# Cross network on one Trainium2 core: first rows in four transfers over two queues, biases on GpSimd's queue, small turns later

## The chip, the cores and the metric

The kernel runs on one core of one Trainium2 chip. A core has five engines with instruction streams of their own: TensorE (PE, matrix products into PSUM, with weight loads shown apart as PEld), VectorE (DVE), ScalarE (ACT), GpSimd (POOL) and SyncE (SP, which here only issues transfers). They wait for each other through semaphores. SP, ACT and GpSimd can issue DMA transfers between the chip's memory and the core's SBUF. The metric is device time of one execution in microseconds (us), the median of several runs.

## The reference

```python
B, F, D, L = 4096, 26, 16, 6
Din = min(F * D, 1024)                      # 416
# x0: (4096, 416), ws: (6, 416, 416), bs: (6, 416), all bfloat16
def reference(x0, ws, bs):
    x = x0
    for l in range(ws.shape[0]):
        x = x0 * (x @ ws[l] + bs[l]) + x
    return x
```

Six cross layers on 4096 rows of 416 features. Each layer is one 416 x 416 product per row, a bias, a product with the input and a sum.

## The kernel before

The kernel keeps x transposed: features on the 128 partitions, rows along the free dimension. The 416 features are cut into three blocks of 128 (called c, or k as an input and m as an output) and a tail of 32. The 4096 rows are done in NP = 4 passes of 1024, each pass in two blocks of NB = 512 rows. The tails of all 1024 rows of a pass are packed into one tile of 128 x 256, four groups of 32 partitions. A pass goes through the six layers; n = p * L + l counts the 24 steps. In every step TensorE does the products of block 0 (`main(p, l, 0, n)`), the tail's (`tail`, lines 433 to 485) and those of block 1; VectorE adds the bias and multiplies by x0 (L606, L615), with ScalarE (L708) and GpSimd (L290) doing one of the six chunks between them. The sum with x is folded into PSUM: the products of a pass's layers accumulate there, so x0 * (sum + bias) is the next x. The last step (`last`) turns the result so that rows are on the partitions.

The change touches the start, where nothing is in SBUF yet. There the order is written out by hand on each engine:

- **Loading.** Rows 0 to 511 (block 0 of pass 0) come as they lie in memory, in `xin_sb`, four groups j = 0 to 3 of 128 rows. SP loads groups 0 and 1 in one transfer (L162), ACT groups 2 and 3 in another (L648). Then SP issues the weights of layer 0 in three transfers (L166, semaphores `s_w0[k]`), a transposing load of rows 512 to 1023 (L169, `s_x0[0]`), waits for the third weights, and goes on with the weights of the later layers (L174, L178). ACT goes on with the tails of rows 512 to 1023 (L651, `xtb_sb`), the biases (L655, `bsa_sb`, after GpSimd has filled that tile with ones) and the tail's weight rows of layer 0 (L656, `w3_sb`).
- **Constants.** GpSimd makes `ones_sb`, `bsa_sb`, the identity `ident`, `u_sb` and a zeroed `wc_sb` (L245 to L256), then packs the tails into `xtn_sb` (L261, two copies, counted by `s_xtp`), copies the tail biases (L270, `s_bs4`) and builds the block-diagonal `wc_sb` (L277).
- **TensorE.** `idle(28)` issues 28 products of a constant (L309) whose result nobody reads. Then `first()` turns `xin_sb` by column block: for c = 0, 1, 2 the four groups j (L321), waiting for the two loads in c = 0; `at(c, j)` names the PSUM bank. `s_inT` counts what is ready: both halves of c = 0, then c = 1, then c = 2. Then come the products of layer 0 for k = 0, 1, 2 (L381, four each, 512 or 256 columns), each k after its weights and after VectorE's copy of that column block. Behind k = 0 stand the two small turns, which transpose the packed tails (L353), and the four bias products (`biases`, L332), which put the biases of all layers on the partitions. `tail` of step 0 (L458, then L391 and L479) waits for the copied tails, `cb_sb`, the full `w3_sb` and, ahead of L479, for the transposing load.
- **VectorE.** Four copies of the turned blocks (L580, `s_ev` 1 to 4), the copy of the turned tails (L585, `s_ev` 5) and two half copies of it (L588, `s_dup`), the copy of the biases to `cb_sb` (L590, `s_cb`), and a copy inside `w3_sb` (L595, `s_w30`). Then the steps.

## Time and profile before

| | us |
|---|---|
| median of 3 runs | 129.04 (128.87 to 129.15) |
| the profiled execution's own time | 128.59 |
| its span, first to last instruction | 126.8 |
| TensorE busy | 123.3 (97%) |
| VectorE busy | 93.3 (74%) |
| ScalarE busy | 45.1 (36%) |
| GpSimd busy | 32.1 (25%) |

The profile records one execution. The time of an execution is a little longer than its span, since it takes in what lies around the instructions. In the views a line of the timeline gives start, length, engine, line of the kernel, operation, what it writes and reads, and the number of instructions merged into it; "SPq" and "ACTq" are instructions that issue transfers. The chain is the work that ended last, followed back from the end. "L321" is line 321 of the kernel before; most line numbers behind the change differ from it in the kernel after.

### The profile page before, as it was taken

What the parts mean: (1) busy time and instruction counts of PE and PEld (TensorE: products, weight loads), DVE (VectorE), ACT (ScalarE), POOL (GpSimd) and SP (SyncE); (2) the same over time, 40 slices, a digit from 0 to 9 for tenths busy, and PEclk for the clock granted to TensorE, in tenths of its full rate; (3) what the DMA queues carried; (4) which work ended last, traced back from release to release, by engine and by line L of the source; (5) the groups of instructions that cost most, each with busy time, mean ns of one, the idle gap of its engine ahead of it and who ended that gap; (6) DMA issues with size and microseconds to landing.
All of it is one profiled execution on the core that took longest, in us unless ns stands there. A gap on an engine that the chain in (4) does not pass through costs nothing.

```text
span 126.8 us, 5809 instructions
## 1 busy us (share of the span) xinstructions
PE 123.3 (97%) x2930; PEld 65.7 (52%) x2403; DVE 93.3 (74%) x156; ACT 45.1 (36%) x99; POOL 32.1 (25%) x42
## 2 busy tenths in 40 slices
PE   7999999999999999999999999999999999999991
PEld 7754554554554554555445545545545545545571
DVE  0567967868869769669669679688687696696873
ACT  0544724625422413403404314224214224135720
POOL 5351311312303303303303213123033033033040
PEclk9999999999999999999999999999999999999999
DMA  3969999597899304907001968000000768000017
GB/s 106 255 157 309 203 119 169 68 100 171 246 120 153 60 16 82 177 20 254 0 16 20 119 130 269 5 0 5 5 10 16 139 114 269 5 0 5 0 53 221
DMA packets 35623, 13.27 MB, mean 105 GB/s; under 512 B 26986, under 2 KB 35600, under 8 KB 35600
## 3 DMA queue, kind: packets, MB, share of 16 engines
q1 hardware_dynamic: 33912, 12.07, 48.4%
q10 hardware_dynamic: 1688, 0.83, 2.5%
q8 instruction: 21, 0.34, 1.1%
q14 instruction: 2, 0.02, 0.0%
HBM read 3.99 MB, written 3.41 MB: 58 GB/s over the span
## 4 chain that ended last, share of the span: by engine, by line
PE 95%; DVE 3%; DVEq 0%; issue 0%
PE ps L391 62%; PE ps L371 11%; PE ps L458 8%; PE ps L479 6%; PE ps L381 4%; PE ps L309 2%; DVE o_sb L635 2%; PE ps L321 1%; PE ps L552 0%; DVE o_sb L641 0%; DVE x0t_sb L585 0%; DVEq L41 0%; PE ps L353 0%; DVEq L632 0%
## 5 line engine op out<-in xcount | busy, mean ns | idle before, releaser
L606 DVE SCALAR_TENSOR_TENSOR xT_sb<-ps,cb_sb,x0T_sb 128x512 bf16<-128x512 f32 x100 | 69.3, 743 | 22.1 <-PE ps L458 22.1
L391 PE MATMUL ps<-xT_sb,w_sb 128*32 128x512 bf16 (+1 forms) x1380 | 75.7, 343 | 0.0
L391 PEld LDWEIGHTS ps<-xT_sb,w_sb 128*32 128x32 bf16 x1380 | 36.9, 97 | 35.3 <-issue 8.1
L290 POOL TENSOR_TENSOR xT_sb<-t_sb,x0T_sb 128x512 bf16<-128x512 f32 x20 | 23.3, 1163 | 72.1 <-ACT t_sb L708 72.1
L708 ACT ACTIVATE t_sb<-ps,cb_sb 128x512 f32<-128x512 f32 x23 | 15.8, 687 | 59.1 <-PE ps L458 59.1
L371 PE MATMUL ps<-xT_sb,w_sb 128*32 128x256 bf16 x444 | 26.6, 273 | 0.0
L672 ACT ACTIVATE xt_sb<-xt_sb 64x256 bf16<-64x256 bf16 x38 | 15.8, 415 | 9.8 <-DVE xt_sb L615 9.3
L391 PE MATMUL ps<-x0T_sb,w_sb 128*32 128x512 bf16 (+1 forms) x252 | 14.1, 344 | 0.0
L606 DVE SCALAR_TENSOR_TENSOR xo_sb<-ps,cb_sb,x0T_sb 128x512 bf16<-128x512 f32 x15 | 10.4, 744 | 3.3 <-PE ps L458 3.3
L391 PEld LDWEIGHTS ps<-x0T_sb,w_sb 128*32 128x32 bf16 x252 | 6.7, 97 | 6.5 <-issue 1.5
L458 PE MATMUL ps<-xt_sb,w_sb 32*128 32x256 bf16 x228 | 9.6, 271 | 0.0
L479 PE MATMUL ps<-xT_sb,w_sb 128*32 128x256 bf16 x228 | 9.5, 273 | 0.0
L615 DVE SCALAR_TENSOR_TENSOR xt_sb<-ps,cb_sb,x0t_sb 128x256 bf16<-128x256 f32 x20 | 9.5, 474 | 0.0
L458 PEld LDWEIGHTS ps<-xt_sb,w_sb 32*128 32x128 bf16 x228 | 4.2, 92 | 6.2 <-issue 6.1
L290 POOL TENSOR_TENSOR xo_sb<-t_sb,x0T_sb 128x512 bf16<-128x512 f32 x3 | 3.5, 1166 | 11.2 <-ACT t_sb L708 11.2
L479 PEld LDWEIGHTS ps<-xT_sb,w_sb 128*32 128x32 bf16 x228 | 6.1, 97 | 0.1
L391 PE MATMUL ps<-xt_sb,wc_sb 128*32 128x256 bf16 x76 | 5.6, 283 | 0.0
L381 PE MATMUL ps<-w_sb,xT_sb 128*128 128x416 bf16 (+2 forms) x27 | 5.2, 320 | 0.0
L666 ACT ACTIVATE wc_sb<-w_sb 32x32 bf16<-32x32 bf16 x20 | 4.5, 226 | 1.6 <-DMA w_sb<-in_ws_dram 1.2
L371 PE MATMUL ps<-x0T_sb,w_sb 128*32 128x256 bf16 x84 | 5.0, 273 | 0.0
L580 DVE COPY x0T_sb<-ps 128x256 bf16<-128x256 bf16 (+1 forms) x4 | 1.3, 356 | 4.3 <-PE ps L321 4.3
L391 PEld LDWEIGHTS ps<-xt_sb,wc_sb 128*32 128x32 bf16 x76 | 1.9, 92 | 4.0 <-issue 4.0
(56 smaller groups left out, 49.8 us busy)
## 6 DMA issues: line engine op xcount, KB each, us to landing
out_dram<-o_sb SPq DMA_DIRECT2D x3, 832.0 KB, 4.2
w_sb<-in_ws_dram SPq DMA_DIRECT2D x5, 312.0 KB, 5.9
xr_sb<-in_x_dram SPq DMA_DIRECT2D x1, 832.0 KB, 6.1
w_sb<-in_ws_dram SPq DMA_DIRECT2D x5, 104.0 KB, 3.2
out_dram<-o_sb SPq DMA_DIRECT2D x2, 208.0 KB, 2.1
w_sb<-in_ws_dram ACTq DMA_DIRECT2D x3, 104.0 KB
xin_sb<-in_x_dram SPq DMA_DIRECT2D x1, 208.0 KB, 2.9
xin_sb<-in_x_dram ACTq DMA_DIRECT2D x1, 208.0 KB, 3.2
```

What stands on the lines that cost most here:

```text
L290: pool.tensor_tensor(out=xdst(p, l, 0, 2), in0=t_sb[:, n % 2, :], in1=x0c(p, 0, 2), op=ALU.mult,).then_inc(s_pl, 1)
L309: pe.matmul(ps[:, 0, 0:128], lhsT=ones, rhs=ones, start=True, stop=True)
L371: return pe.add_instruction(mybir.InstMatmult(name="I-%d" % (1000000 + count[0]), engine=mybir.EngineType.PE, start_tensor_calc=start, sto ...
L381: return pe.matmul(out, lhsT=lhsT, rhs=rhs, start=start, stop=stop, skip_group_check=True)
L391: ins = pe.matmul(out[c:c + 32, :], lhsT=lhsT[:, c:c + 32], rhs=rhs, start=start, stop=stop, skip_group_check=True, tile_position=(0, c),)
L458: ins = pe.matmul(part(blk, m, h ^ other), lhsT=w3_sb[32 * g:32 * g + 32, l, m * 128:(m + 1) * 128], rhs=xt[32 * g:32 * g + 32, other, :], ...
L479: ins = pe.matmul(ps_tail[32 * g:32 * g + 32, :], lhsT=w_sb[:, l, k, DF:D], rhs=xsrc(p, l, g % 2, k)[:, (g // 2) * NT:(g // 2 + 1) * NT], ...
L606: dve.scalar_tensor_tensor(out=halves(xdst(p, l, blk, c)), in0=chunk2(blk, c), scalar=cb_sb[:, c, l:l + 1], in1=halves(x0c(p, blk, c)), op ...
L615: dve.scalar_tensor_tensor(out=tdst(p, l), in0=ps_tail, scalar=cb_sb[:, 3, l:l + 1], in1=x0t_sb[:, p, 0, :], op0=ALU.add, op1=ALU.mult,).t ...
L666: act.activation(out=wc_sb[gs, l, gs], in_=w3_sb[gs, l, DF:D], func=ACTF.Copy).then_inc(s_wc, 1)
L672: act.activation(out=o, in_=i, func=ACTF.Copy).then_inc(s_dup, 1)
L708: act.activation(out=halves(t_sb[:, n % 2, :]), in_=chunk2(0, 2), func=ACTF.Identity, bias=cb_sb[:, 2, l:l + 1],).then_inc(s_act, 1)
```

## The change

The first 512 rows come in four transfers of 128 rows, groups 0 and 2 on SP and 1 and 3 on ACT, each with a semaphore of its own, ahead of everything else on these queues. TensorE issues 23 products of the constant instead of 28 and turns by group: groups 0 and 1 in all three column blocks as they land, then groups 2 and 3 block by block. The biases are loaded from GpSimd's queue, right after GpSimd has filled their tile with ones and ahead of its other constants. The two small turns move from behind k = 0 to the middle of k = 1, the bias products behind k = 1. On VectorE the copy inside `w3_sb` comes ahead of the copy to `cb_sb`.

```diff
-        s_xin = [sem("s_xin%d" % i) for i in range(2)]
+        s_xin = [sem("s_xin%d" % i) for i in range(4)]
...
         def _(sp):
-            sp.dma_start(
-                xin_sb[:, 0:2, :], x0[0:256, :].rearrange("(j b) d -> b j d", b=128)
-            ).then_inc(s_xin[0], 16)
+            for j in (0, 2):
+                sp.dma_start(xin_sb[:, j, :], x0[j * 128:j * 128 + 128, :]).then_inc(s_xin[j], 16)
...
         def _(pool):
+            pool.memset(bsa_sb[:, :], 1.0).then_inc(s_setup, 1)
+            pool.wait_ge(s_setup, 1)
+            pool.dma_start(bsa_sb[1:L + 1, :], bs[:, :]).then_inc(s_bs, 16)
             pool.memset(ones_sb[:, :], 1.0).then_inc(s_ones, 1)
-            pool.memset(bsa_sb[:, :], 1.0).then_inc(s_setup, 1)
             pool.wait_ge(s_ones, 1)
...
-            idle(28)
+            idle(23)
             pe.wait_ge(s_setup, 3)
...
-            def turn(c):
-                for j in range(4):
-                    if c == 0 and j % 2 == 0:
-                        pe.wait_ge(s_xin[j // 2], 16)
+            def turns():
+                order = [(j, c) for j in range(2) for c in range(3)]
+                order += [(j, c) for c in range(3) for j in range(2, 4)]
+                for j, c in order:
+                    if c == 0:
+                        pe.wait_ge(s_xin[j], 16)
                     ins = pe.transpose(
                         out=psT[:, at(c, j), j * 128:(j + 1) * 128],
                         in_=xin_sb[:, j, c * 128:(c + 1) * 128], identity=ident[:, :],
                     )
-                    if c == 0 and j == 1:
+                    if (j, c) == (1, 0) or j == 3:
                         ins.then_inc(s_inT, 1)
+            def small_tails():
+                pe.wait_ge(s_xtp, 2)
+                for c in range(2):
+                    ins = pe.transpose(
+                        out=psT[:, 2, c * 128:(c + 1) * 128],
+                        in_=xtn_sb[:, 0, c, :], identity=ident[:, :],
+                    )
                 ins.then_inc(s_inT, 1)
...
             def first():
-                for c in range(3):
-                    turn(c)
+                turns()
                 for k in range(3):
                     pe.wait_ge(s_w0[k], 16)
                     pe.wait_ge(s_ev, k + 2)
                     for m in range(3):
                         for o, x in pieces(0, m, xsrc(0, 0, 0, k)):
                             whole(o, w_sb[:, 0, k, m * 128:(m + 1) * 128], x, k == 0, False)
-                    if k == 0:
-                        pe.wait_ge(s_xtp, 2)
-                        for c in range(2):
-                            ins = pe.transpose(
-                                out=psT[:, 2, c * 128:(c + 1) * 128],
-                                in_=xtn_sb[:, 0, c, :], identity=ident[:, :],
-                            )
-                        ins.then_inc(s_inT, 1)
+                        if (k, m) == (1, 1):
+                            small_tails()
+                    if k == 1:
                         biases()
...
         def _(dve):
...
+            dve.wait_ge(s_w30, 1)
+            dve.tensor_copy(
+                out=w3_sb[64:128, 0, DH:D], in_=w3_sb[0:64, 0, DH:D]
+            ).then_inc(s_w30, 1)
             dve.wait_ge(s_inT, 6)
             dve.tensor_copy(
                 out=cb_sb[:, :, :],
                 in_=ps[:, 7, D:D + 32].rearrange("p (c e) -> p c e", e=8)[:, :, 0:L],
             ).then_inc(s_cb, 1)
-            dve.wait_ge(s_w30, 1)
-            dve.tensor_copy(
-                out=w3_sb[64:128, 0, DH:D], in_=w3_sb[0:64, 0, DH:D]
-            ).then_inc(s_w30, 1)
...
         def _(act):
-            act.dma_start(
-                xin_sb[:, 2:4, :], x0[256:512, :].rearrange("(j b) d -> b j d", b=128)
-            ).then_inc(s_xin[1], 16)
+            for j in (1, 3):
+                act.dma_start(xin_sb[:, j, :], x0[j * 128:j * 128 + 128, :]).then_inc(s_xin[j], 16)
             act.dma_start(
                 xtb_sb[:, :, :], x0[NB:2 * NB, DF:D].rearrange("(j b) d -> b j d", b=128)
             ).then_inc(s_xtb, 16)
-            act.wait_ge(s_setup, 1)
-            act.dma_start(bsa_sb[1:L + 1, :], bs[:, :]).then_inc(s_bs, 16)
             act.dma_start(w3_sb[0:DR, 0, :], ws[0, DF:D, :]).then_inc(s_wt[0], 16)
```

## The prediction

> **What bounds the kernel now.** I read the page first: busy shares, then the chain.
>
> ```profile
> PE 123.3 (97%) x2930; PEld 65.7 (52%) x2403; DVE 93.3 (74%) x156; ACT 45.1 (36%) x99; POOL 32.1 (25%) x42
> ...
> PE 95%; DVE 3%; DVEq 0%; issue 0%
> ```
>
> TensorE is busy for 97% of the span and carries 95% of the chain that ends last. From the first layer's tail rows (L458) on, nothing but TensorE sets the pace, so a start that reaches L458 earlier or later by d moves the end by d. The change touches only the first 8 us. I therefore read the timeline of each engine there; first TensorE's (start, length, line, tiles, count):
>
> ```profile
> 0.83 3.15 PE L309 MATMUL ps<-const-bfloat16-1.0 128*128 128x128 bf16 x28 [0.83 <-PEq L751]
> 3.84 1.19 PE L321 MATMUL ps<-ident,xin_sb 128*128 128x128 bf16 x12
> 4.90 0.81 PE L381 MATMUL ps<-x0T_sb,w_sb 128*128 128x512 bf16 x4
> 5.55 0.27 PE L353 MATMUL ps<-ident,xtn_sb 128*128 128x128 bf16 x2
> 5.83 0.23 PE L332 MATMUL ps<-u_sb,bsa_sb 128*128 128x6 bf16 x3
> ...
> 6.16 1.24 PE L381 MATMUL ps<-x0T_sb,w_sb 128*128 128x512 bf16 x7
> 7.33 0.51 PE L458 MATMUL ps<-x0t_sb,w_sb 32*128 32x256 bf16 x12
> ...
> 7.89 0.50 PE L479 MATMUL ps<-x0T_sb,w_sb 128*32 128x256 bf16 x12
> ```
>
> The engine has almost no holes: 28 warming matmuls to 3.84, twelve turns, four products, two small turns, four bias products, eight products (the record of the first, near 5.95, is missing). Only one hole is worth naming: the second small turn starts at 5.60 and is over in the array 0.05 later, and the bias products start at 5.83. That is 0.17 us of waiting for GpSimd's bias copy, which runs from 5.48 to 5.78. Next VectorE, which feeds these steps:
>
> ```profile
> 4.25 1.35 DVE L580 COPY x0T_sb<-ps 128x256 bf16<-128x256 bf16 x4 [4.25 <-PE ps L321]
> 5.86 0.29 DVE L585 COPY x0t_sb<-ps 128x256 bf16<-128x256 bf16 x1 [0.26 <-PE ps L353]
> 6.18 0.47 DVE L588 COPY x0t_sb<-x0t_sb 64x256 bf16<-64x256 bf16 x2
> 6.58 0.17 DVE L590 COPY cb_sb<-ps 128x24 f32<-128x24 f32 x1
> 6.78 0.21 DVE L595 COPY w_sb<-w_sb 64x208 bf16<-64x208 bf16 x1
> ```
>
> Everything L458 needs is done at 6.99, and TensorE comes to it at 7.33: VectorE is 0.34 us ahead. Last the queues and the landings of the first rows:
>
> ```profile
> 0.79 0.46 SPq L162 DMA_DIRECT2D xin_sb<-in_x_dram  x1
> 1.31 1.40 SPq L166 DMA_DIRECT2D w_sb<-in_ws_dram  x3
> 2.75 1.76 SPq L169 DMA_TRANSPOSE x0T_sb<-in_x_dram  x1
> ...
> 1.86 0.65 ACTq L655 DMA_DIRECT2D bsa_sb<-in_bs_dram  x1
> ...
> 1.67 0.19 POOL L252 TENSOR_SCALAR_AFFINE_SELECT u_sb<-ones_sb 128x6 bf16<-128x6 bf16 x1
> ...
> L321 PE MATMUL ps<-ident,xin_sb x12: 219/282/314, 3.8 to 4.8; 128*128 128x128 bf16 x12
> ...
> DMA to landing us min/median/max: 2.9/3.0/3.2
> ```
>
> The two loads of first rows land at 0.79 + 2.9 = 3.7 and 0.80 + 3.2 = 4.0. The turns cost 0.107 each at first and 0.056 at the end (TensorE's pace doubles at about 4.6, although the granted clock is printed as 1.00 throughout; the 314 and 219 ns in the row are the same fact).
>
> **The change, part by part.** Let S be the first turn (3.84 now), T the first product (4.90 now), E the start of L458 (7.33 now).
>
> *Five warming matmuls fewer, rows in quarters.* 5 x 0.107 = 0.53, so S = 3.31 if a quarter is there. The first quarter holds half the bytes of the load that lands at 3.7, on the same queue. Between 3.7 (no gain from halving) and the 2.9 less half of the 1.8 from the queue's first packets to landing, so 2.8, I take 3.1: not the gate. The last quarter is behind the same bytes as before, so it lands at 4.0. Its issue starts at 1.3 and takes 0.45 to 0.49, while the queues are still moving the first quarters, so the extra issue itself delays no row; what it delays is priced under SP's queue.
>
> *Turning by quarters.* Product k=0 needs the turns of all four quarters of column block 0. They were turns 1 to 4; now the fourth of them is turn 8. Spacing: the second turn follows at 0.06 (3.84 to 3.90), later ones at 0.107: 3.31 + 0.06 + 6 x 0.107 = 4.01, plus a hundredth or two for waits, 4.03. The landing bound gives the same, 4.0 + 0.04. From the fourth turn's start now (4.11) to the copy's start (4.46) is 0.35, the copy takes 0.29, TensorE follows 0.05 to 0.15 later (4.75 to 4.90 now, still turning until 4.87); I take 0.10. T = 4.03 + 0.74 = 4.77, **0.13 earlier**. Of the 0.53 saved ahead, 0.40 is given back.
>
> *SP's queue.* Weights and the transposing load are issued one issue (0.47) later. The bytes ahead of the first weights are the same, so I take their 4.4 (1.31 + 3.1); the bad end is 4.87, which would make T 4.92. Second weights: 5.0 to 5.5, wanted at T + 0.65 = 5.42. Third: 6.1 to 6.55, wanted at 6.29; they wait under the stall found below. The transposing load: 2.75 + 0.47 + 4.5 = 7.72, wanted by L479 at E + 0.56; cover shrinks from 0.64 to 0.2, cost nothing as long as that holds. Layer 1's weights land later than these and have over a microsecond of slack (9.1 against 10.1).
>
> *Biases on GpSimd's queue, ahead of its constants.* ACT loses an issue of 0.65 and gains one of about 0.47: nothing waits there. GpSimd does bsa_sb first (0.45), then issues, then makes ones, ident and u_sb (0.79 to 1.86 now, less the 0.45: about 0.7 from ones to the end). No DMA is issued from GpSimd in this trace. Bounds: 0.33 (the cheapest issue on ACT) and 1.76 (the dearest on SP); the nearest row is the same transfer's 0.65 on ACT, which I take. The constants are then ready at 1.29 + 0.65 + 0.7 = 2.64, well ahead of 3.31; up to an issue of 1.2 it is hidden. The biases' landing has 0.9 us of cover.
>
> *Small turns and biases later.* The 0.17 hole goes. But VectorE's chain starts later against TensorE: small turns start at T + 0.65 + 0.43 = 5.85, the second at 5.90. VectorE starts 0.26 after that (6.16), copy and two half copies take the 0.80 they take now (5.86 to 6.66): 6.96. The w3 copy 0.03 + 0.21: 7.20. cb after it: 0.17, less the 0.08 by which it now starts ahead of its predecessor's end: 7.29 (7.40 at worst). TensorE sees it 0.05 later and loads: E = 7.36. TensorE alone would be there at T + 3 x 0.65 + 0.11 + 0.12 + 0.10 = 7.04. So **0.32 us of new waiting** stands where the 0.17 hole was.
>
> *Sum.* T -0.13, hole -0.17, wait +0.32, rounding +0.01: E = 7.36, +0.03 us. The profiled execution took 128.59 with a span of 126.8 (1.79 around it), so it would take 128.62. The median of the runs shown is 0.45 above the profiled one; on it the forecast is 129.07, say 129.1. No change, in short: 0.2% is 0.26 us, about what a measurement of this kernel can tell.
>
> **The rivals.**
> *A: VectorE is not late.* If the copies pack more tightly, or L458's wait ends on something earlier, E is TensorE's 7.04, or 6.99 with T at the early end: -0.3 to -0.35 us, 128.7. For it: cb already overlaps its predecessor. Against: the half copies each start 0.03 after the one before, and all are in one order on one engine.
> *B (slower): GpSimd's issue holds the constants.* From an issue of 1.2 us on, each tenth moves S, T and E by a tenth. At 1.76: 129.07 + 0.56 = 129.6. For it: GpSimd's own rows are slow (1.16 us for L290). Against: only six rows.
> *C: the transposing load or the weights come late.* A landing 0.5 later than taken makes L479 wait 0.3; first weights at 4.87 cost 0.16. Together with the forecast: 129.3 to 129.5.
> *D: TensorE's pace doubles later.* Now it needs 3.8 us from the first warming matmul. With fewer of these, more turns and a short wait before T, the count may start over at S: 3.31 + 3.8 = 7.1, and the work between 4.77 and 7.1 runs at half pace, 1.2 us lost, 130.2. For it: turns are then 40% of the stretch instead of 20%. Against: 0.8 us of turns before the present doubling did not prevent it. Beside this the Trainium skill, TensorE: Matmul & The Clock Gate, Part 4: PE-mode transpose, states that transposes do not count as activity for the clock. No run here shows it; by that rule 130.2 would be the likelier time.
>
> **How the numbers follow.** Forecast 0.33 (its own range 128.9 to 129.3), A 0.26, B 0.18, C 0.14, D 0.09. A is faster by over 0.2%; B and D are slower, and two thirds of C. So faster 0.26, within 0.2% 0.33 + 0.05 = 0.38, slower 0.18 + 0.09 + 0.09 = 0.36. The range goes from 128.65, the early end of A, to 129.6, the upper end of B; D, a tenth of A and a little of B are left out.
>
> **What would show it.** First turn near 3.3, first product near 4.8; the small turns near 5.85; the bias read as VectorE's last step before L458, ending near 7.3, and 0.2 to 0.3 us of idle TensorE ahead of L458; no wait ahead of L479. Wrong if VectorE is done before TensorE arrives (A), if turning starts after 3.4 although rows have landed (B), if L479 waits for the transposing load (C), or if products of 512 columns follow at 0.43 instead of 0.215 (D).

## The result and the profile after

The kernel after takes 130.10 us (median of 7 runs, 129.84 to 130.41) against 129.04 us before (7 runs beside it, 128.34 to 129.65): a ratio of 1.0091 with a 95% interval of 1.0068 to 1.0114. It is slower by about 0.9%, where no change was forecast. The profiled execution of after took 129.90 us with a span of 127.9 us; before it was 128.59 with 126.8.

First the page of after, its busy shares and the chain that ended last:

```profile
PE 123.3 (96%) x2926; PEld 65.3 (51%) x2398; DVE 93.5 (73%) x156; ACT 45.1 (35%) x99; POOL 32.8 (26%) x43
...
PE 89%; DVE 4%; DMA 2%; issue 2%; POOL 0%; ACTq 0%; DVEq 0%; POOLq 0%
```

TensorE is busy as long as before, 123.3 us, in a span 1.1 us longer. The chain now has transfers and GpSimd in it: TensorE waits for something that it did not wait for before. The timeline of TensorE shows where (start, length, line, operation, number of instructions merged, and in brackets the idle time before and what ended it):

```profile
3.33 1.44 PE L325 MATMUL ps<-ident,xin_sb 128*128 128x128 bf16 x12
5.30 1.26 PE L387 MATMUL ps<-x0T_sb,w_sb 128*128 128x512 bf16 x6 [0.53 <-DMA w_sb<-in_ws_dram]
6.68 0.28 PE L335 MATMUL ps<-ident,xtn_sb 128*128 128x128 bf16 x2
6.81 0.38 PE L387 MATMUL ps<-x0T_sb,w_sb 128*128 128x256 bf16 x2
...
7.13 0.81 PE L387 MATMUL ps<-x0T_sb,w_sb 128*128 128x512 bf16 x4
8.36 0.51 PE L464 MATMUL ps<-x0t_sb,w_sb 32*128 32x256 bf16 x12 [0.42 <-DVE cb_sb L600]
...
8.92 0.28 PE L485 MATMUL ps<-x0T_sb,w_sb 128*32 128x256 bf16 x4
```

The first turn comes at 3.33 (3.84 before), the first product at 5.30 (4.90), the tail rows at 8.36 (7.33). The tail rows are 1.03 later, and that is nearly all of the longer span (1.1): from their start to the end it is 119.51 us before and 119.55 after. Three waits stand ahead of them, for the first weights, for the small turns' input, and for the biases' copy. The view of waits, of the first 9 us, names them (total, times, longest):

```profile
POOL xtn_sb L262 <- DMA xtb_sb<-in_x_dram: 2.0, 1, 2.0
...
PEld ps L387 <- DMA w_sb<-in_ws_dram: 0.8, 1, 0.8
...
PEld ps L335 <- POOL xtn_sb L262: 0.6, 1, 0.6
```

GpSimd stood 2.0 us waiting for the transfer of the tails (`xtb_sb`), and TensorE for GpSimd. The engines that issue transfers and GpSimd's own timeline, and the row of the tails' tile:

```profile
0.80 0.86 SPq L163 DMA_DIRECT2D xin_sb<-in_x_dram  x2
1.71 1.37 SPq L165 DMA_DIRECT2D w_sb<-in_ws_dram  x3
...
1.72 0.46 ACTq L656 DMA_DIRECT2D xtb_sb<-in_x_dram  x1
...
1.54 0.75 POOL L246 DMA_DIRECT2D bsa_sb<-in_bs_dram  x1 [0.30 <-POOL bsa_sb L244]
...
2.85 0.18 POOL L253 TENSOR_SCALAR_AFFINE_SELECT u_sb<-ones_sb 128x6 bf16<-128x6 bf16 x1
...
6.34 0.29 POOL L262 COPY xtn_sb<-xtb_sb 128x128 bf16<-128x128 bf16 x1 [1.95 <-DMA xtb_sb<-in_x_dram]
...
DMA to landing us min/median/max: 4.6/4.6/4.6
```

Before, the same issue, the copy that waits for it, and the tile's row were:

```profile
1.32 0.50 ACTq L651 DMA_DIRECT2D xtb_sb<-in_x_dram  x1
...
4.64 0.29 POOL L261 COPY xtn_sb<-xtb_sb 128x128 bf16<-128x128 bf16 x1 [0.23 <-DMA xtb_sb<-in_x_dram]
...
DMA to landing us min/median/max: 3.3/3.3/3.3
```

The tails were issued 0.40 later than before (1.72 against 1.32), but landed 4.6 us after that instead of 3.3: at 6.29 instead of 4.59. The first weights were issued 0.40 later too (1.71 against 1.31) and landed at 5.25 instead of 4.38; their rows, before and then after:

```profile
DMA to landing us min/median/max: 3.1/3.1/3.1
...
DMA to landing us min/median/max: 3.5/3.5/3.5
```

Last VectorE:

```profile
3.96 1.40 DVE L586 COPY x0T_sb<-ps 128x256 bf16<-128x256 bf16 x4 [3.96 <-PE ps L325]
7.01 0.29 DVE L591 COPY x0t_sb<-ps 128x256 bf16<-128x256 bf16 x1 [1.66 <-PE ps L335]
7.33 0.47 DVE L594 COPY x0t_sb<-x0t_sb 64x256 bf16<-64x256 bf16 x2
7.84 0.21 DVE L596 COPY w_sb<-w_sb 64x208 bf16<-64x208 bf16 x1
8.08 0.18 DVE L600 COPY cb_sb<-ps 128x24 f32<-128x24 f32 x1
```

Its chain from the small turns to `cb_sb` is what the tail rows wait for, as forecast; it only starts 0.85 later (7.01 instead of 6.16).

The queues did less in the same stretch, although as much was waiting in them: up to 3.4 us both kernels had moved about the same, 410 KB before and 406 KB after, by the packets in the traces. Busy time by stretch, of before and then of after; the last two columns are the DMA share and GB/s:

```profile
3.40:4.00 0.60, 0.60 (x8) 0.44 (x5) 0.00 (x0) 0.60 (x1) 0.00 (x0) 1.00 1.27 274
4.00:4.60 0.60, 0.60 (x8) 0.58 (x7) 0.35 (x2) 0.39 (x2) 0.29 (x1) 1.00 1.15 324
```

```profile
3.40:4.00 0.60, 0.60 (x8) 0.59 (x8) 0.04 (x1) 0.60 (x1) 0.31 (x1) 1.00 0.88 151
4.00:4.60 0.60, 0.60 (x8) 0.50 (x5) 0.47 (x3) 0.24 (x2) 0.29 (x1) 1.00 0.82 172
```

Up to 3.4 us the rows (416 KB) are on the move in both. Then, when weights and tails should flow, the kernel after moves 151 and 172 GB/s where the kernel before moved 274 and 324.

### The profile page after: what moved, and what is told of

Same layout as the page of the kernel before. It is cut to its first block, busy times and chain, and to the rows that moved or that the text cites. A ratio compares the mean times of both kernels' runs of the same rounds, so it can differ in the third digit from the quotient of the medians.

```text
span 127.9 us, 5803 instructions
## 1 busy us (share of the span) xinstructions
PE 123.3 (96%) x2926; PEld 65.3 (51%) x2398; DVE 93.5 (73%) x156; ACT 45.1 (35%) x99; POOL 32.8 (26%) x43
## 4 chain that ended last, share of the span: by engine, by line
PE 89%; DVE 4%; DMA 2%; issue 2%; POOL 0%; ACTq 0%; DVEq 0%; POOLq 0%
PE ps L397 61%; PE ps L377 11%; PE ps L464 8%; PE ps L485 6%; DVE o_sb L641 2%; DMA xin_sb<-in_x_dram 2%; PE ps L387 2%; POOL xtn_sb L262 0%; PE ps L558 0%; DVE o_sb L647 0%; DVE x0t_sb L594 0%; ACTq L655 0%; DVE x0t_sb L591 0%; PE ps L335 0%; DVE w_sb L596 0%
## 5 line engine op out<-in xcount | busy, mean ns | idle before, releaser
L485 PE MATMUL ps<-xT_sb,w_sb 128*32 128x256 bf16 x228 | 9.5, 273 | 0.0
L485 PEld LDWEIGHTS ps<-xT_sb,w_sb 128*32 128x32 bf16 x228 | 6.1, 97 | 0.1
```

Source lines behind the costliest of these rows:

```text
L485: ins = pe.matmul(ps_tail[32 * g:32 * g + 32, :], lhsT=w_sb[:, l, k, DF:D], rhs=xsrc(p, l, g % 2, k)[:, (g // 2) * NT:(g // 2 + 1) * NT], ...
```

## The experiments

The question was why the same weights and tails land so much later. The theories that were tried: GpSimd's new transfer slows the others; the short packets of the tails (64 bytes each) meet the weights; four transfers instead of two do it as such; and, when that had held, whether it is the place on the queue (weights and tails are third on theirs, not second) or the time of their issue. Where an expectation names a theory by a letter, G is the first of these, X the second, S the third, and I and L belong to the last question; Q and N are explained where they come up. Beside each ratio stands the interval; landings are those of the profiled execution, from the trace.

**Biases back on ACT's queue.** The kernel after without GpSimd's transfer:

```diff
-            pool.memset(bsa_sb[:, :], 1.0).then_inc(s_setup, 1)
-            pool.wait_ge(s_setup, 1)
-            pool.dma_start(bsa_sb[1:L + 1, :], bs[:, :]).then_inc(s_bs, 16)
             pool.memset(ones_sb[:, :], 1.0).then_inc(s_ones, 1)
+            pool.memset(bsa_sb[:, :], 1.0).then_inc(s_setup, 1)
...
+            act.wait_ge(s_setup, 1)
+            act.dma_start(bsa_sb[1:L + 1, :], bs[:, :]).then_inc(s_bs, 16)
             act.dma_start(w3_sb[0:DR, 0, :], ws[0, DF:D, :]).then_inc(s_wt[0], 16)
```

> The changed kernel with one part undone: the biases are loaded from ACT's queue again, behind the tails of rows 512 to 1023, and GpSimd issues nothing. Theory G (the transfer issued by GpSimd slows the transfers that are under way beside it, from about 3.6 us on): the first weights land by 4.5 us instead of 5.26, the tails by 4.8 instead of 6.29; the first product starts near 4.8, the tail rows of step 0 near 7.4, the ratio to the kernel before is 0.999 to 1.001. Theory Q (the order on the two hardware queues does it: the tails' 512 short packets now stand behind two transfers and meet the weights): landings stay at about 5.2 and 6.2, the tail rows start near 8.3, ratio 1.007 to 1.010.

Measured: 1.0079 (1.0048 to 1.0109). First weights 5.18, tails 6.40, tail rows 8.47. TensorE's lines show the same waits:

```profile
5.23 1.26 PE L385 MATMUL ps<-x0T_sb,w_sb 128*128 128x512 bf16 x6 [0.41 <-DMA w_sb<-in_ws_dram]
6.80 0.28 PE L333 MATMUL ps<-ident,xtn_sb 128*128 128x128 bf16 x2 [0.31 <-POOL xtn_sb L260]
```

GpSimd's transfer is not the cause; the loss stays without it.

**The biases on GpSimd's queue alone**, in the kernel before:

```diff
+            pool.memset(bsa_sb[:, :], 1.0).then_inc(s_setup, 1)
+            pool.wait_ge(s_setup, 1)
+            pool.dma_start(bsa_sb[1:L + 1, :], bs[:, :]).then_inc(s_bs, 16)
             pool.memset(ones_sb[:, :], 1.0).then_inc(s_ones, 1)
-            pool.memset(bsa_sb[:, :], 1.0).then_inc(s_setup, 1)
...
-            act.wait_ge(s_setup, 1)
-            act.dma_start(bsa_sb[1:L + 1, :], bs[:, :]).then_inc(s_bs, 16)
```

> The kernel before with one part of the change alone: GpSimd fills the biases' tile first and loads the biases from its own queue; rows still come in two transfers, turns, small turns and biases stand where they stood. Theory G: the first weights land at 5.0 or later (4.39 before), the tails at 5.5 or later (4.59), the tail rows of step 0 start 0.6 to 1.0 us later than 7.33, ratio 1.005 to 1.009. Theory Q: landings as before within 0.2 us, ratio 0.999 to 1.001.

Measured: 1.0024 (1.0003 to 1.0045). First weights 4.42 and tails 4.63 as before; the biases, on the queue that GpSimd issues, land at 5.55, and GpSimd waits 0.6 us for them ahead of its copy. By itself this move costs about a quarter of the loss, at the edge of what the runs can tell.

**Small turns early again**: the run before last, with the small turns behind k = 0 as in the kernel before, to see whether their place matters.

```diff
-                        if (k, m) == (1, 1):
+                        if (k, m) == (0, 2):
                             small_tails()
```

> As the first of these kernels (biases on ACT's queue), and the two small turns stand behind k = 0 again, while the bias products stay behind k = 1. Theory G with the prediction's VectorE chain: the first product near 4.8, the copies of the turned tails end near 6.6 and the bias copy near 6.9, so nothing waits ahead of the tail rows, which start near 7.05; ratio 0.997 to 0.998. Theory Q: the small turns wait for the late tails wherever they stand, the tail rows start near 8.3, ratio 1.007 to 1.010.

Measured: 1.0045 (1.0023 to 1.0067). The tails land at 6.40, so the small turns come at 6.80 wherever they stand in the order; TensorE now idles 0.79 ahead of them and the tail rows are at 8.48. In the comparison over many executions it is about 0.3% better than the last but one run and below Q's 1.007, though the intervals overlap.

**Tails last on ACT's queue**, so that their short packets come after the weights (otherwise as in the first run):

```diff
-            act.dma_start(
-                xtb_sb[:, :, :], x0[NB:2 * NB, DF:D].rearrange("(j b) d -> b j d", b=128)
-            ).then_inc(s_xtb, 16)
             act.wait_ge(s_setup, 1)
             act.dma_start(bsa_sb[1:L + 1, :], bs[:, :]).then_inc(s_bs, 16)
             act.dma_start(w3_sb[0:DR, 0, :], ws[0, DF:D, :]).then_inc(s_wt[0], 16)
+            act.dma_start(
+                xtb_sb[:, :, :], x0[NB:2 * NB, DF:D].rearrange("(j b) d -> b j d", b=128)
+            ).then_inc(s_xtb, 16)
```

> The changed kernel with the biases on ACT's queue, and the tails of rows 512 to 1023 issued last on that queue, behind the biases and the tail's weight rows. Theory X (the tails' 512 packets of 64 B run beside the first weights, because both queues now finish the rows together, and the two slow each other): the first weights land by 4.6 us instead of 5.2, the first product starts near 4.8; the tails land between 5.0 and 6.0 and set the small turns; the tail rows of step 0 start between 7.4 and 8.0, ratio 1.001 to 1.006. Theory S (four transfers instead of two are the cause, whatever stands behind them): the first weights still land at 5.0 or later.

Measured: 1.0088 (1.0073 to 1.0103). The first weights land at 5.14 without the tails beside them, so the tails' packets do not hold them up. The tails, issued a whole microsecond later, land at 6.47 instead of 6.40.

**Four transfers alone.** The kernel before with nothing changed but the number of transfers:

```diff
-            sp.dma_start(
-                xin_sb[:, 0:2, :], x0[0:256, :].rearrange("(j b) d -> b j d", b=128)
-            ).then_inc(s_xin[0], 16)
+            for j in (0, 1):
+                sp.dma_start(xin_sb[:, j, :], x0[j * 128:j * 128 + 128, :]).then_inc(s_xin[0], 16)
...
-                        pe.wait_ge(s_xin[j // 2], 16)
+                        pe.wait_ge(s_xin[j // 2], 32)
...
-            act.dma_start(
-                xin_sb[:, 2:4, :], x0[256:512, :].rearrange("(j b) d -> b j d", b=128)
-            ).then_inc(s_xin[1], 16)
+            for j in (2, 3):
+                act.dma_start(xin_sb[:, j, :], x0[j * 128:j * 128 + 128, :]).then_inc(s_xin[1], 16)
```

> The kernel before with the rows in four transfers of 128 rows (groups 0 and 1 on SP, 2 and 3 on ACT), each pair counted by one semaphore; TensorE's order, the 28 warming products and the biases stay. Theories S and X: the rows land by 4.0 as before, but the first weights at 5.0 or later (4.39 before) and the tails at 5.8 or later (4.59); the tail rows of step 0 start near 8.3, ratio 1.006 to 1.010. If splitting does nothing (then the new order of turns or the queues' assignment of groups would have to): landings within 0.2 us of before, ratio 0.999 to 1.001.

Measured: 1.0097 (1.0075 to 1.0120), the whole loss. First weights 5.22, tails 6.12:

```profile
5.27 1.19 PE L380 MATMUL ps<-x0T_sb,w_sb 128*128 128x512 bf16 x4
6.52 0.28 PE L352 MATMUL ps<-ident,xtn_sb 128*128 128x128 bf16 x2
...
8.26 0.51 PE L457 MATMUL ps<-x0t_sb,w_sb 32*128 32x256 bf16 x12
```

The split of the rows is enough for the loss; the new order of turns, the biases' queue and the later small turns are not needed for it.

**Tails behind the biases**, in the kernel before with its two transfers; only the tails are third on their queue, issued at 1.99:

```diff
+            act.wait_ge(s_setup, 1)
+            act.dma_start(bsa_sb[1:L + 1, :], bs[:, :]).then_inc(s_bs, 16)
             act.dma_start(
                 xtb_sb[:, :, :], x0[NB:2 * NB, DF:D].rearrange("(j b) d -> b j d", b=128)
             ).then_inc(s_xtb, 16)
-            act.wait_ge(s_setup, 1)
-            act.dma_start(bsa_sb[1:L + 1, :], bs[:, :]).then_inc(s_bs, 16)
```

> The kernel before with the tails of rows 512 to 1023 issued behind the biases on ACT's queue, about 0.5 us later than before; rows still in two transfers. Theory X: the tails now meet the first weights without any splitting, the first weights land at 4.7 or later and the tails at 5.5 or later; the tail rows of step 0 start at 7.8 or later, ratio above 1.003. Theory S: the first weights land at 4.4 as before, the tails by 5.1, and the tail rows start within 0.2 us of 7.33, ratio 0.999 to 1.002.

Measured: 1.0062 (1.0042 to 1.0081). First weights 4.37 as before, tails 6.16:

```profile
6.56 0.28 PE L353 MATMUL ps<-ident,xtn_sb 128*128 128x128 bf16 x2 [0.30 <-POOL xtn_sb L261]
...
8.30 0.51 PE L458 MATMUL ps<-x0t_sb,w_sb 32*128 32x256 bf16 x12
```

Late tails alone make two thirds of the loss, with no row split at all. Neither theory had this: X expected late weights as well, S neither late.

**Biases ahead of the weights on SP**: the weights third, issued at 1.82, tails second as before.

```diff
+            sp.wait_ge(s_setup, 1)
+            sp.dma_start(bsa_sb[1:L + 1, :], bs[:, :]).then_inc(s_bs, 16)
             for k in range(3):
...
-            act.wait_ge(s_setup, 1)
-            act.dma_start(bsa_sb[1:L + 1, :], bs[:, :]).then_inc(s_bs, 16)
```

> The kernel before with the biases' transfer moved from ACT's queue to SP's, between the rows and the first weights; rows still in two transfers. This issues the weights and the transposing load about 0.6 us later without splitting anything. Theory L (with two transfers SP's queue runs about 0.35 us ahead of ACT's and starts the weights while ACT's queue still moves rows, so the slow first reads of the weights are covered; with four the queues finish the rows together and the cover is gone): the first weights land by 4.7 us. Theory I (the later issue of the weights is what delays them): they land at 5.0 or later, and the tail rows of step 0 start at 7.8 or later, ratio above 1.004.

Measured: 1.0019 (0.9997 to 1.0041). First weights 5.37, tails 4.35. L, which had the weights by 4.7, falls. I holds for the landing but not for the price: late weights alone cost about 0.2%, with an interval from nothing to 0.4%.

**Only ACT's rows in two, only SP's rows in two**, in the kernel before (the waits for the rows are changed to fit):

```diff
...
-            act.dma_start(
-                xin_sb[:, 2:4, :], x0[256:512, :].rearrange("(j b) d -> b j d", b=128)
-            ).then_inc(s_xin[1], 16)
+            for j in (2, 3):
+                act.dma_start(xin_sb[:, j, :], x0[j * 128:j * 128 + 128, :]).then_inc(s_xin[1], 16)
```

> The kernel before with only ACT's rows split (two transfers of 128 rows; SP keeps its one of 256). Theory L: SP's queue still runs ahead, the first weights land by 4.6, ratio 0.999 to 1.003 (the tails, issued 0.4 later behind two transfers, may land late and cost some of that). Theory I: weights are issued at 1.31 as before, so they land by 4.6 as well. Theory N (the number of transfers in flight as such): a loss half as large as with four, the first weights at about 4.8.

```diff
-            sp.dma_start(
-                xin_sb[:, 0:2, :], x0[0:256, :].rearrange("(j b) d -> b j d", b=128)
-            ).then_inc(s_xin[0], 16)
+            for j in (0, 1):
+                sp.dma_start(xin_sb[:, j, :], x0[j * 128:j * 128 + 128, :]).then_inc(s_xin[0], 16)
...
```

> The kernel before with only SP's rows split (two transfers of 128 rows; ACT keeps its one of 256). Theory L: ACT's queue starts earlier against SP's, SP's lead is lost, the first weights land at 5.0 or later. Theory I: the weights are issued 0.4 later, also 5.0 or later; the run with the biases on SP's queue tells L from I. Theory N: about 4.8. The tails, issued at 1.3, land by 4.8 in L and I.

Measured: ACT's split 1.0061 (1.0036 to 1.0086), tails 6.51, first weights 4.32; SP's split 1.0015 (0.9993 to 1.0036), tails 4.59, first weights 4.96. Each split makes late what stands behind it on its own queue, and it is ACT's queue, with the tails, that costs. N, which had the first weights at about 4.8 in both, falls. In the traced execution of SP's split the late weights are not what the first product waits for: TensorE, at half pace until 6.82, was turning up to that product, at 5.50.

**Rows on ACT.** The kernel of the third run with first weights second on SP, tails third there, and three row transfers on ACT:

```diff
-            for j in (0, 2):
-                sp.dma_start(xin_sb[:, j, :], x0[j * 128:j * 128 + 128, :]).then_inc(s_xin[j], 16)
+            sp.dma_start(xin_sb[:, 0, :], x0[0:128, :]).then_inc(s_xin[0], 16)
...
+                if k == 0:
+                    sp.dma_start(
+                        xtb_sb[:, :, :], x0[NB:2 * NB, DF:D].rearrange("(j b) d -> b j d", b=128)
+                    ).then_inc(s_xtb, 16)
...
-            for j in (1, 3):
+            for j in (1, 2, 3):
                 act.dma_start(xin_sb[:, j, :], x0[j * 128:j * 128 + 128, :]).then_inc(s_xin[j], 16)
-            act.dma_start(
-                xtb_sb[:, :, :], x0[NB:2 * NB, DF:D].rearrange("(j b) d -> b j d", b=128)
-            ).then_inc(s_xtb, 16)
```

> The changed order of turns with small turns behind k = 0, biases on ACT's queue, and the queues arranged so that SP leads: SP moves the first quarter, the first weights, the tails and the other weights, ACT the other three quarters, the biases and the tail's weight rows. Theory L: the first weights land by 4.5 although there are four transfers, the rows by 4.2; the first product starts between 4.8 and 5.0, the tails land by 5.0, the tail rows of step 0 start between 7.0 and 7.3, ratio 0.996 to 1.000. Theories I and N: the first weights are issued at 1.3, so I allows this as well; N expects 5.0 or later and a ratio above 1.004.

Measured: 1.0082 (1.0048 to 1.0115). The first weights, issued at 1.25, land at 3.83, the earliest of all; group 3 of the rows, issued at 1.72, lands at 5.67, and the wait for it is TensorE's:

```profile
PE ps L326 <- DMA xin_sb<-in_x_dram: 1.4, 1, 1.4
```

So it does not matter what is loaded: rows become as late as weights and tails. Here too, third place and issue after 1.7 came together.

**The order part alone.** The kernel before with small turns in k = 1, biases behind k = 1, and the copy in `w3_sb` first:

```diff
-                    if k == 0:
-                        pe.wait_ge(s_xtp, 2)
...
+                        if (k, m) == (1, 1):
+                            pe.wait_ge(s_xtp, 2)
...
+                    if k == 1:
                         biases()
...
```

> The kernel before with the order part of the change alone: small turns in the middle of k = 1, bias products behind k = 1, the w3 copy ahead of the copy to cb_sb; loads as before. If the loss lies in the four transfers alone, the prediction's own sum holds here: first product 4.90, small turns 4.90 + 0.65 + 0.43 = 5.98, VectorE's copies from 6.24 to 7.04, w3 to 7.28, cb to 7.37, tail rows at 7.44 instead of 7.33, with some 0.3 us of waiting for VectorE's cb copy: +0.1 us, ratio 1.001 (within 0.2%). If the later small turns carry a part of the loss of their own (VectorE's chain longer than reckoned), tail rows at 7.8 or later and a ratio of 1.004 to 1.009. If VectorE packs tighter (rival A), tail rows at 7.16 and a ratio of 0.9987.

Measured: 1.0023 (0.9997 to 1.0049). Tails at 4.77, no wait for them, yet the tail rows come at 7.84:

```profile
6.48 0.29 DVE L586 COPY x0t_sb<-ps 128x256 bf16<-128x256 bf16 x1 [0.97 <-PE ps L353]
6.81 0.47 DVE L589 COPY x0t_sb<-x0t_sb 64x256 bf16<-64x256 bf16 x2
7.31 0.21 DVE L591 COPY w_sb<-w_sb 64x208 bf16<-64x208 bf16 x1
7.55 0.18 DVE L595 COPY cb_sb<-ps 128x24 f32<-128x24 f32 x1
...
7.84 0.51 PE L459 MATMUL ps<-x0t_sb,w_sb 32*128 32x256 bf16 x12 [0.42 <-DVE cb_sb L595]
```

That is 0.40 later than the 7.44 of the sum: 0.08 from the first product (4.98, not 4.90), 0.11 from the small turns (6.17 is 1.19 behind the first product, not 1.08; the second weights landed at 5.68), 0.05 from the turns to VectorE's copy (0.31 for 0.26), 0.12 from `cb_sb`, which starts 0.03 after its predecessor's end instead of 0.08 ahead of it, and the rest from small gaps. The wait for VectorE is real and somewhat dearer than forecast, but the kernel is not measurably slower for it; the interval leaves room for the 0.5 us by which the tail rows of this trace are later than 7.33.

**Biases behind k = 1 only**, small turns left behind k = 0, with the copy in `w3_sb` first as in the run before:

```diff
                         ins.then_inc(s_inT, 1)
+                    if k == 1:
                         biases()
...
```

> The kernel before with the bias products behind k = 1 and the w3 copy ahead of the copy to cb_sb; the small turns stay behind k = 0. The hole of 0.17 us ahead of the bias products goes, and VectorE's chain of small-turn copies starts as before (5.86) and ends with w3 at about 6.9 and cb at about 7.03. If the prediction's reading of the hole is right, tail rows start at 7.16 with no wait: -0.17 us, ratio 0.9987 (128.9). If VectorE is late after all, at 7.2 to 7.3 and a ratio of 0.9995 to 1. If the loads of this start vary from run to run by more than that, no difference can be seen.

Measured: 0.9997 (0.9970 to 1.0024). From first product to tail rows it is 2.32 (5.04 to 7.36) instead of 2.43, no wait stands ahead of the tail rows, and the hole ahead of the bias products is gone. But the two further profiles of the kernel before (below) have 2.30 and 2.32 as well, and no hole: there GpSimd's bias copy starts at 5.00 and 4.99, without a wait, where in the first profile it waited for the biases until 5.48. The hole of 0.17 belongs to one execution, and there is nothing to gain from it in the others. This was the one candidate for beating the kernel before, and no gain can be measured.

**Weights second, but later.** The kernel before with a wait ahead of SP's first weights; the place on the queue is kept. The first waits on too early a signal, the second on all of GpSimd's constants:

```diff
+            sp.wait_ge(s_setup, 1)
             for k in range(3):
```

> The kernel before with SP waiting, between its rows and the first weights, for GpSimd's memset that ACT's biases wait for as well: the weights stay second on SP's queue, the bytes and packets are the same, but they are issued at about 1.8 instead of 1.31. If the place on the queue decides (third and later transfers are slow), the first weights land 3.1 us after their issue, at 4.9, with hardly any packets over 300 ns; first product at 5.0, ratio 1.001 to 1.002. If the time of issue decides (whatever is issued after about 1.7 is slow), they land at 5.2 to 5.4 as in the kernel after, with ten or so long packets; first product at 5.3 to 5.4, ratio 1.003 to 1.009. Tails stay second on ACT and should land at about 4.6 either way.

```diff
+            sp.wait_ge(s_setup, 3)
             for k in range(3):
```

> As the run before it, which held the first weights up by 0.1 us only (issued at 1.41): here SP waits for all of GpSimd's first constants, so that the weights are issued at about 1.88, half a microsecond later than before and later than they were in the kernel with four transfers (1.71); they stay second on SP's queue. If the place on the queue decides, the first weights land at 4.4 to 5.0 with hardly any long packets, the tails at 4.6; first product at 4.9 to 5.05, ratio 0.999 to 1.001. If the time of issue decides, the first weights land at 5.2 or later with ten or so long packets, first product at 5.3 or later, ratio 1.003 to 1.009. In both cases the second and third weights are issued half a microsecond later than before and may land later for that.

Measured: the first was issued at 1.41, only 0.1 later, with weights at 4.43 and a ratio of 0.9990 (0.9965 to 1.0016): it tells nothing. The second was issued at 1.88 and landed at 5.10, between what the two theories expected; ratio 1.0020 (0.9999 to 1.0041). The long packets do not tell either: of SP's 832-byte packets between 3.0 and 4.8 us, three took over 300 ns, against none or one in the three profiles of the kernel before and seven and five in the two of the kernel after. For the weights this did not decide.

**Tails second, but later**, the same wait on ACT ahead of the tails:

```diff
+            act.wait_ge(s_setup, 3)
             act.dma_start(
                 xtb_sb[:, :, :], x0[NB:2 * NB, DF:D].rearrange("(j b) d -> b j d", b=128)
             ).then_inc(s_xtb, 16)
```

> The kernel before with ACT waiting for GpSimd's first constants between its rows and the tails: the tails stay second on ACT's queue, but are issued at about 1.88 instead of 1.32, later than in the kernel after (1.72). If the place on the queue makes them slow, they land 3.0 to 3.4 us after their issue as in the kernel before, at 4.9 to 5.3, the small turns start at 5.55 to 5.8, tail rows at 7.33 to 7.5 and the ratio is 1.000 to 1.002. If the time of issue does (whatever is issued after about 1.7 is slow), they land 4.2 to 4.6 after it, at 6.1 to 6.5, tail rows start at 8.2 to 8.5 and the ratio is 1.005 to 1.007.

Measured: 1.0085 (1.0053 to 1.0116). ACT's issue, the tails' row, and TensorE:

```profile
1.89 0.40 ACTq L652 DMA_DIRECT2D xtb_sb<-in_x_dram  x1
...
DMA to landing us min/median/max: 4.1/4.1/4.1
...
6.42 0.28 PE L353 MATMUL ps<-ident,xtn_sb 128*128 128x128 bf16 x2 [0.40 <-POOL xtn_sb L261]
...
8.26 0.51 PE L458 MATMUL ps<-x0t_sb,w_sb 32*128 32x256 bf16 x12
```

Second on their queue, behind one row transfer of full size, and still landing at 6.02: their place on their own queue is not the cause for the tails. The later issue is, or something that goes with it (see Not settled, below). Of this execution's loss 0.39 us stands behind the tail rows: from their start to the end it is 119.90 us, where it is 119.5 to 119.6 in 17 of the twenty traces (the other two are ACT's split, 119.78, and the biases back on ACT's queue, 120.00); the profile does not name what is waited for there. With this run the landings of all twenty traces fall into two groups (issue and landing in us):

| | issued | landed | traces |
|---|---|---|---|
| tails | 1.30 to 1.32 | 4.27 to 4.77 | 10 |
| tails | 1.71 to 2.69 | 5.79 to 6.51 | 10 |
| first weights | 1.25 to 1.41 | 3.83 to 4.58 | 11 |
| first weights | 1.70 to 1.88 | 4.96 to 5.38 | 9 |

No trace has an issue between, so where the step lies, or whether it is one, is not known.

**The unchanged kernels again.** Executions of one kernel differ by up to 1.5 us (before: 128.59 to 130.09 in the 29 runs beside the order part alone), and the traces differ in one more thing, the time at which TensorE's pace doubles (products of 128 columns then follow each other at 56 ns instead of 107). Two more profiles of the kernel before and one of the kernel after, no edit:

> The kernel before, unchanged, looked at a second time, to see what differs between executions of one kernel (they went from 128.4 to 130.1 us). In the traces so far TensorE's pace doubles at times between 3.84 and 6.82 us, whatever the kernel. If that is a matter of the execution, the doubling comes here at any time in that stretch, and the time follows it: each 0.1 us after 4.6 costs 0.05, so a span of 126.8 at 4.6 or earlier and of 127.7 at 6.4, while tails land at 4.3 to 4.8 and first weights at 4.4 either way. If instead the loads make the difference between executions, the doubling stays at about 4.6 and a longer span goes with tails or weights that land half a microsecond or more later.

> A third look at the kernel before, with the same expectations as the second: the time of the doubling sets the span (126.8 at 4.6 or earlier, 127.7 at 6.4), loads as before; or, if the loads make the difference, a doubling at about 4.6 and a longer span with late loads.

> The kernel after, unchanged, looked at a second time. If the place on the queue makes the tails late, they land at 6.1 or later again and the tail rows start at 8.2 to 8.6 wherever the pace doubles between 3.8 and 6.8, since TensorE waits for the tails in any case; span 127.8 to 128.5. If the first look was a chance of one execution, tails land at 4.6 to 5, tail rows start at 7.4 to 7.6 and the span is about 127.0.

Measured: before 128.61 and 128.74, tails 4.71 and 4.62, tail rows 7.26 and 7.36, doubling at 4.29 and 4.97 (4.64 in the first profile). Neither was one of the longer executions of this kernel, so they do not say what makes those longer. After 131.29, weights 5.38, tails 6.32, so the late landings belong to the kernel; but here the pace doubled only at 9.90 (5.17 in the first profile):

```profile
5.42 2.31 PE L387 MATMUL ps<-x0T_sb,w_sb 128*128 128x512 bf16 x6 [0.57 <-DMA w_sb<-in_ws_dram]
...
9.70 0.47 PE L464 MATMUL ps<-x0t_sb,w_sb 32*128 32x256 bf16 x8
```

The six products that took 1.26 us take 2.31, and the tail rows start at 9.70, later than any theory expected.

## Why the prediction was wrong, step by step

**Right.** The first turn (forecast 3.31, seen 3.33), the landing of the last quarter (4.0; 3.94), GpSimd's issue (0.65 taken, 0.75 seen) with the constants ready at 3.03 ahead of the first turn, so that rival B did not happen; the transposing load (7.72; 7.68) with no wait ahead of L485; the new wait for VectorE's bias copy as the last before the tail rows (0.32; 0.42); and that a start which reaches the tail rows later moves the end by as much (1.03 and 1.1).

**Wrong: "The bytes ahead of the first weights are the same, so I take their 4.4".** This is the step that failed, here for the weights and in the next paragraph for the tails. It let a later issue cost nothing because the bytes ahead were the same, and its bad end, 4.87, added just the delay of the issue. Seen: 5.25, beyond the bad end. VectorE's second copy was done as reckoned (4.68; forecast 4.67) and TensorE's last turn at 4.77, so the first product lost 0.53 to this one landing. The nearest row by time of issue pointed this way: in the three profiles of the kernel before, the second weights, issued at 1.80 or 1.81 with more bytes ahead, landed at 4.97, 4.98 and 5.51.

**Wrong by leaving it out: the tails.** The sentence on SP's queue priced the later issue for weights and transposing load; the tails, one issue later on ACT for the same reason, appear nowhere. Their cover was in the trace of before: landed at 4.59, GpSimd's copy done at about 4.9, wanted by the forecast at 5.85. A landing at 6.29 is 1.7 later and passes this cover. This is the term that counts most. The first small turn came at 6.68, where first product plus 1.08 would have been 6.38, so 0.30 more on top of the late weights (0.29 of it waiting); against the forecast's 5.85 it is 0.83 later.

**A term that rested on one execution: the hole, -0.17.** In two of the three profiles of the kernel before there is no such hole, as the run with the biases behind k = 1 showed. Without this term the same sum gives +0.20 us instead of +0.03. That the forecast came out at no change was therefore in part luck of the profile it was read from; the measured loss of 1.06 us does not hang on it.

**The sum again, from 7.36 to 8.36**: first weights 0.53, tails 0.29, `cb_sb` 0.12 (it did not overlap its predecessor; the 7.40 named as worst was the better value: in all twelve traces where this copy follows the half copies it starts 0.08 ahead of the end of the last, and in all eight where it follows the copy in `w3_sb` 0.03 behind that one's end), and 0.06 in gaps of 0.01 to 0.03. The two landings overlap, by the same sum: with the weights on time, tails at 6.29 would still have held the small turns at 6.68 and the tail rows at 8.36. The runs agree with this: the late tails alone cost 0.6 to 0.85% (tails behind the biases, ACT's split, tails second but later) and the late weights alone 0.15 to 0.2% (biases ahead of the weights, SP's split, weights second but later; no interval is clear of zero).

**Rivals.** C named weights at 4.87 and a price of 0.16: the right mechanism, too short a reach, since its bound was the shift of the issue and not what the queues do with it; and it does not name the tails. A fell with VectorE's wait. D is not what made the first profile slow (there the pace doubled at 5.17, ahead of the first product), but it exists: in the second profile it doubled at 9.90, later than D's 7.1, and that execution, at 131.29, is 1.2 us above the median of 130.10, which is D's price. The rule that stood beside D, the Trainium skill's TensorE: Matmul & The Clock Gate, Part 4, that transposes do not count as activity, is neither shown nor refuted by these runs: of two executions of the same instructions one doubled at 5.17 and one at 9.90.

**Not settled.** Why an issue 0.4 to 0.6 us later moves the tails' landing by 1.0 to 2.2. Two rivals fit the traces as well as the time of issue does. One is the place in the order of issue over all queues together: in all twenty traces, tails and first weights that landed early were the third or fourth transfer issued, and those that landed late the fifth or a later one. No run parts this from the time. The other, for the tails, is the transposing load: in the ten traces with early tails all their 512 packets start ahead of that load's first packet (the last at 3.88 to 4.31 us, that packet at 4.31 to 4.73); in the ten with late tails 19 to 320 of them start behind it. It can't be all of it: in the kernel after its first packet starts at 4.86, and the queues moved half as much already between 3.4 and 4.0, as the windows above show. Taking the transposing load away from this stretch was not tried. The Trainium skill, DMA: Bandwidth & Descriptors, section "Issuing engines are not separate DMA queues", states that transfers of all issuing engines run on the same 16 DMA engines and interleave. In the kernel after, transfers on both queues land late (weights 5.25, tails 6.29), which agrees with that. It does not give the step, and with one queue split only the one of the two that stood behind the split was late (tails 6.51 beside weights 4.32; weights 4.96 beside tails 4.59).

## What to carry to other kernels

A transfer put ahead of others costs these one issue each, and the landing behind it can move by several times that (here 0.40 us of issue, 0.87 for the weights and 1.70 for the tails): price every transfer behind it on both queues against the step that wants it, and not only the one that the change is about. Splitting a load gains only what starts on its first part; here the turns started 0.5 us earlier; 0.4 of that went, as forecast, into turning the last quarter, and the rest and more into waits for what had been pushed behind. Before a profiled start is compared with another, see when TensorE's pace doubles in each, and profile each more than once: the hole that the forecast closed was there in one of three.

## What the hardware showed that was not expected

The two groups of landings: tails issued at 1.30 to 1.32 us landed at 4.27 to 4.77, and issued at 1.71 to 2.69 at 5.79 to 6.51, ten traces each; an issue at 2.69 landed at 6.47, those at 1.71 to 1.74 at 5.79 to 6.51. It was the same for third place on its queue and for second; what else goes with it stands under Not settled.

The doubling of TensorE's pace: warming starts at 0.83 in every kernel, and the doubling came between 3.84 and 6.82 us in 16 of the 17 traces that record it, and at 9.90 in one, where TensorE had waited for weights and tails. The three profiles of the kernel before gave 4.29, 4.64 and 4.97. A late one is dear. In the run with SP's rows in two, which doubled at 6.82, four products took

```profile
5.50 1.47 PE L380 MATMUL ps<-x0T_sb,w_sb 128*128 128x512 bf16 x4
```

and in the second profile of the kernel before, which doubled at 4.29,

```profile
4.96 0.81 PE L381 MATMUL ps<-x0T_sb,w_sb 128*128 128x512 bf16 x4
```

(the lengths run to the modelled end of the last product). The profiled executions of the two runs with late weights, doubling at 6.45 and 6.82, took 129.47 and 129.71 us, where other executions of the same kernels took as little as 128.71 and 128.58, so a good part of the spread of one kernel's executions would be this; that was seen in these few traces and not tested. The Trainium skill, TensorE: Matmul & The Clock Gate, Part 1, states that the clock is decided in free-running windows of about 3.4 us, so that the moment varies by 0.5 us either way from run to run. That it varies agrees, and the three moments of the kernel before lie within that; the 3.84 to 6.82 seen here is wider, though over different kernels, and the 5.17 and 9.90 of the kernel after are wider still.
